# Attention backward on one core: the last 104 heads taken in pairs, with 16 KB rows in the transfers

## The chip, the core and the metric

The kernel runs on one core of one Trainium2 chip. The metric is device time in microseconds, the median of several executions: 1704.82 us for the kernel before. One core has TensorE (PE), VectorE (DVE), ScalarE (ACT), GpSimd (POOL) and a sync engine (SP) that here does nothing but issue transfers; 16 DMA engines move data between memory (HBM) and the on-chip buffer (SBUF), which has 128 partitions.

## What is computed

A decoder block with one query token for each of 4 sequences, forward, and then the gradients of all inputs. Cut to what matters:

```python
# B=4, H=32, Sk=4096, Dh=128: 128 heads (b, h), each with K and V of 4096 x 128 bf16 = 1 MB
q = layernorm(x) @ wq
p = softmax(q @ K^T * Dh**-0.5)           # one row of 4096 for each head
o = p @ V
h = x + o @ wo
out = h + swiglu(layernorm(h), w1, w3, w2)
# backward, for each head, with dO (1 x 128) from grad_out:
dV = outer(p, dO)                          # 4096 x 128, 1 MB
dP = dO @ V^T                              # needs V again
dS = p * (dP - sum(dO * o)) * Dh**-0.5     # one row of 4096
dK = outer(dS, q)                          # 4096 x 128, 1 MB
# and dx, d_wq, d_wo, d_w1, d_w2, d_w3
```

Both cache gradients are outer products of a column of 4096 and a row of 128, so the kernel writes 256 MB of dK and dV and reads K once and V twice, 384 MB.

## The kernel before, in words

A head is numbered s, with b = s % 4 and h = s // 4. In SBUF a head lies as 128 partitions x 32 rows of 128 elements: partition p has cache rows 32p to 32p+31, 8 KB in one run, so a transfer of one head is 128 rows of 8 KB. All large buffers come from one `arena` of 23 slots of 8,320 bytes a partition. `Slot` takes the first of the list `free`, `give` puts it back at its end; both happen while the program is written, so the list decides which earlier transfer a new user of a slot has to wait for. `Slot2` takes two neighbouring slots, for the 2 MB stores of weight gradients.

The forward part fills about the first 680 us. It streams K and V (L155, L163), keeps the probabilities in `P_all` (for each head 32 values a partition) and some sums for each head in the `M` slots, of which there are 8 when the backward part begins.

The backward part is one loop over s. Its order is written by hand; each engine takes its instructions in that order, and SP issues its transfers one after the other, each when its semaphores allow. In one step of the loop:

- `load_ahead(s + L)` (L1233) and `prefetch` (L1209) issue V loads (L810). V uses a ring `vring` of 7 slots; a load goes out as soon as a ring slot has been given back.
- `front(s + L)` (L1166), five heads ahead: 32 PE transposes of V (L777) in 4 groups, each evacuated by ACT onto the place of V (L778); then 8 matmuls (L1182) with dO in one column of a window `zd` of zeros, which GpSimd sets (L1147). Four heads share an accumulator `dP_ps`. At the next head after four `rows_out` copies it (L1157) and `rows_T` transposes it (L1164).
- `more_V(s + 1 + lead_V(s))`: dV of heads up to 8 ahead of s, from head 56 on gradually fewer, to 3. `grad_V` (L790) takes a slot, lets DVE write the outer product (`outer`, L783) and stores it (L794). Its inputs are the row dO, replicated on all partitions by PE and ACT four heads at a time (`replicate`, L1133 and L1136), and P with each value twice, side by side, from GpSimd (`P_pairs`, L1152).
- `grad_K(s)` (L1202): the same for dK, store L1206. Its column comes from `group_dS` (L1190) on DVE, once for four heads: four small subtractions (L1196) and one product with P (L1199).
- one or two units of other work (`step`): first the rest of dO (`rest_of_dO`), then one dq matmul for each head (`dq_work`), which gives back the M slots one by one, and from s = 35 on `side_work`: dx and the weight gradients, whose seven stores of about 2 MB (L1045) take 16 KB or 14 KB a partition.

The core of the slot and of one store:

```python
class Slot:
    def __init__(self, name, src=free):
        self.i = src.popleft()
...
def grad_K(s):
    gk = Slot("gk")
    outer(gk.heads(), dS2s[s // B][:, s % B], reps["rq", s // REP][:, s % REP, :])
    nc.sync.dma_start(out=rows_of(out_2[b, h]), in_=gk.heads())
    gk.give()
```

Of the kernel before, what the change touches and what calls it, by code (L numbers as in the profile page):

```python
# [9 lines left out]
FP32 = mybir.dt.float32  # L10
# [9 lines left out]
JQ = 8  # L20
NPE = 1


@with_exitstack
def kernel(
# [79 lines left out]

    free = deque(range(NSLOT))
    arena = slotp.tile([P, NSLOT * SLOT], BF16, name="arena")

    class Slot:
        def __init__(self, name, src=free):  # L110
            self.i = src.popleft()
            self.t = arena[:, self.i * SLOT:(self.i + 1) * SLOT]
# [10 lines left out]
        def give(self):  # L123
            free.append(self.i)

    class Slot2:
        def __init__(self):
            at = {i: n for n, i in enumerate(free)}
            self.i = min((max(at[i], at[i + 1]), i) for i in free if i + 1 in at)[1]
            free.remove(self.i)  # L130
            free.remove(self.i + 1)
            self.t = arena[:, self.i * SLOT:(self.i + 2) * SLOT]
# [673 lines left out]
    def load_V2(eng=nc.sync):  # L806
        s = nv["next"]
        if s < NH:
            V2s[s] = Slot("V2", vring if vring else free)
            eng.dma_start(out=V2s[s].heads(), in_=cache_head(A_v_cache, s))  # L810
            nv["next"] += 1
# [128 lines left out]
    with ExitStack() as c2:  # L940
# [204 lines left out]
        def dO_window(s):  # L1145
            if s < NH:
                nc.gpsimd.tensor_copy(out=zd[s % B][:, 32:132:67], in_=dOT_bf[:, s:s + 1].to_broadcast([P, 2]))  # L1147

        def P_pairs(s):
            if s < NH and s not in P2s:  # L1150
                P2s[s] = bw3.tile([P, SJ, 2], BF16, tag="P2", name="P2")
                nc.gpsimd.tensor_copy(out=P2s[s][:], in_=P_all[:, s, :, None].to_broadcast([P, SJ, 2]))  # L1152
# [13 lines left out]
        def front(s):  # L1166
# [20 lines left out]
            sl = VTs.pop(s)  # L1187
            (vring if len(V2s) + len(VTs) + len(vring) < NV2 else free).append(sl.i)

# [19 lines left out]
        def prefetch():  # L1209
            while nv["next"] < NH and vring:  # L1210
                load_V2(nc.sync)


        O0, S0, S1, L = 2, 21, 35, 5
        gvd = {"n": 2}

        def more_V(upto):
            while gvd["n"] < min(NH, upto):
                s = gvd["n"]
                P_pairs(s)  # L1220
                replicate("rdo", s - s % REP)
                grad_V(s)
                P_pairs(s + 1)
                P_pairs(s + 2)
                gvd["n"] += 1
                if s % REP == 2:
                    replicate("rdo", s + 2)

        def lead_V(s):
            return 8 - min(5, max(0, s - 56) // 4)  # L1230


        def load_ahead(s):  # L1233
            prefetch()
            if s < NH and s not in V2s and s not in VTs:
                load_V2(nc.sync)

        for s in range(2):
            dO_window(s)
# [11 lines left out]
        group_dS(0)  # L1251
        for s in range(NH):
            load_ahead(s + L)
            if s % REP == 2:
                replicate("rq", s + 2)
            if s + L < NH:
                front(s + L)
            elif s + L == NH:
                rows_out()
                rows_T()  # L1260
            if s > 0:
                more_V(s + 1 + lead_V(s))
            grad_K(s)
            if s % B == B - 1 and s + 1 < NH:
                group_dS((s + 1) // B)
            if O0 <= s < S0:
                step("o")
            if s >= S1:
                step("s", 2)
            elif s >= O0:  # L1270
                step("q")
        step("s", 400)
# [30 lines left out]
```

## Time and profile before

| | |
|---|---|
| time | 1704.82 us, three runs from 1703.26 to 1705.42 |
| profiled span | 1701.5 us |
| busy | PE 1235.3, DVE 1236.1, ACT 969.0, POOL 377.3 us |
| moved | 707.50 MB, HBM read 422.59 MB, written 282.34 MB |
| DMA packets on the main queue | 100,144 |
| outer products on DVE (L783) | 2292 ns each |
| evacuation of V groups on ACT (L778) | 1026 ns each, 512 of them |

The page gives for each engine the busy time, then the span in 40 equal slices with a busy digit for each engine, the DMA engines' mean busy share and the rate in GB/s. A share just over 1 for DMA means that packets of one engine overlap slightly. Groups of instructions stand with their count, busy time, mean duration, and the idle time of the engine just before them with what ended it. A busy PE is not a PE at its peak. For a transfer, "to landing" is the time from its issue by SP to its completion.

### The profile page before, as it was taken

The numbers are of one execution on the slowest core, as the hardware profiler recorded it, in microseconds if no ns is written. First come the engines' busy times: TensorE is split into PE (matmuls) and PEld (weight loads), VectorE is DVE, ScalarE is ACT, GpSimd is POOL, SyncE is SP. The second block draws the span as 40 slices with busy tenths as digits, with TensorE's granted clock in tenths as the row PEclk, the third lists the DMA queues.
The fourth block names the chain that finished last, engine by engine and source line by source line (L and its number), as shares of the span: only waits on it lengthen the run. The fifth ranks groups of instructions, "written<-read, shape, count | busy, mean of one in ns | idle before, by whom it ended". The sixth has DMA issues, their size and how long they took to land. (4 is left out here: it accounts for less than half of the span.)

```text
span 1701.5 us, 38421 instructions
## 1 busy us (share of the span) xinstructions
PE 1235.3 (73%) x16180; PEld 913.6 (54%) x16180; DVE 1236.1 (73%) x1294; ACT 969.0 (57%) x1502; POOL 377.3 (22%) x678
## 2 busy tenths in 40 slices
PE   5889888888888888878877664676557666766650
PEld 4777776667666766655655443444334343434430
DVE  5989999999999987667776666664457555665682
ACT  3555444544454444776666564677457865766540
POOL 1211222222222221233341111141114121200020
PEclk9999999999999999999999897979787977787775
DMA  9999999999999999999999999999999999999996
GB/s 401 424 424 424 424 424 424 424 423 424 417 423 412 424 405 400 385 420 424 425 426 425 425 426 425 425 426 427 423 425 420 417 422 412 414 416 420 411 424 275
DMA packets 100733, 707.50 MB, mean 416 GB/s; under 512 B 10940, under 2 KB 15176, under 8 KB 16720
## 3 DMA queue, kind: packets, MB, share of 16 engines
q1 hardware_dynamic: 100144, 704.95, 99.4%
q8 instruction: 127, 2.08, 0.5%
q14 instruction: 46, 0.38, 0.1%
q0 software_dynamic: 416, 0.10, 0.0%
HBM read 422.59 MB, written 282.34 MB: 414 GB/s over the span
## 5 line engine op out<-in xcount | busy, mean ns | idle before, releaser
L778 ACT COPY arena<-pt_tps 128x1024 bf16<-128x1024 bf16 x512 | 490.2, 1026 | 185.5 <-PE pt_tps L777 178.9
L777 PE MATMUL pt_tps<-ident_b,arena 128*128 128x128 bf16 x4096 | 351.6, 246 | 199.9 <-ACT arena L778 112.7
L777 PEld LDWEIGHTS <-arena 128*128 128x128 bf16 x4096 | 299.4, 112 | 274.5 <-issue 151.4
L783 DVE TENSOR_TENSOR arena<-P,arena 128x4096 bf16<-128x4096 bf16 x125 | 286.3, 2292 | 196.5 <-DMA out_dram<-arena 178.2
L783 DVE TENSOR_TENSOR arena<-dS,arena 128x4096 bf16<-128x4096 bf16 x128 | 293.1, 2292 | 119.1 <-DMA out_dram<-arena 118.3
L449 PE MATMUL M_ps<-arena 128*128 128x130 bf16 x4096 | 286.6, 223 | 37.6 <-DMA arena<-in_A_v_cache_dram 37.1
L434 DVE TENSOR_TENSOR arena<-arena 128x4096 bf16<-128x4096 bf16 x128 | 292.5, 2285 | 25.3 <-POOL arena L430 25.3
L449 PEld LDWEIGHTS <-arena 128*128 128x128 bf16 x4096 | 253.6, 99 | 58.2 <-DMA arena<-in_A_v_cache_dram 50.5
L341 DVE STREAM_TRANSPOSE arena<-arena 128x512 f32<-128x512 f32 (+1 forms) x321 | 250.5, 797 | 0.0
L336 ACT COPY arena<-pt_tps 128x1024 bf16<-128x1024 bf16 x128 | 129.4, 1012 | 186.4 <-PE pt_tps L335 148.8
L1182 PE MATMUL dP_ps<-arena,zd 128*32 128x512 bf16 x1024 | 175.7, 420 | 71.1 <-ACT arena L778 67.9
L1152 POOL COPY P<-P_all 128x64 bf16<-128x64 bf16 x125 | 82.1, 657 | 523.2 <-DVE arena L783 512.9
L1147 POOL COPY zd<-dOT_bf 128x2 bf16<-128x2 bf16 x128 | 123.4, 966 | 121.8 <-PE dP_ps L1182 121.8
L347 POOL TENSOR_TENSOR W<-qrep,wmask 128x128 bf16<-128x128 bf16 x128 | 120.8, 944 | 85.2 <-PE S_ps L367 70.4
L430 POOL COPY arena<-P_all 128x64 bf16<-128x64 bf16 x128 | 32.4, 253 | 413.8 <-ACT P_all L424 410.8
L1182 PEld LDWEIGHTS <-zd 128*32 128x32 bf16 x1024 | 37.0, 94 | 158.1 <-issue 144.1
L424 ACT COPY P_all<-pt_P 32x64 bf16<-32x64 bf16 x256 | 51.9, 203 | 55.6 <-PE pt_P L420 53.4
L953 ACT CAST arena<-gps 128x512 bf16<-128x512 f32 x110 | 62.7, 584 | 33.0 <-PE gps L959 29.3
L335 PE MATMUL pt_tps<-ident_b,arena 128*128 128x128 bf16 x1024 | 80.6, 224 | 0.0
L459 PE MATMUL kP_ps<-arena,onesw 128*32 128x512 bf16 x1024 | 79.2, 386 | 0.0
L335 PEld LDWEIGHTS <-arena 128*128 128x128 bf16 x1024 | 62.0, 100 | 25.8 <-issue 25.8
L413 ACT ACTIVATE Pn<-E,rl 128x1024 bf16<-128x1024 f32 x64 | 73.7, 1151 | 3.2 <-DVE rl L410 3.2
(226 smaller groups left out, 1190.6 us busy)
## 6 DMA issues: line engine op xcount, KB each, us to landing
arena<-in_A_v_cache_dram SPq DMA_DIRECT2D x256, 1024.0 KB, 18.3
out_dram<-arena SPq DMA_DIRECT2D x256, 1024.0 KB, 20.1
arena<-in_A_k_cache_dram SPq DMA_DIRECT2D x128, 1024.0 KB, 15.5
arena<-in_A_wq_dram SPq DMA_DIRECT2D x8, 1024.0 KB, 15.5
out_dram<-arena SPq DMA_DIRECT2D x4, 2048.0 KB, 22.8
arena<-in_B_w_dram SPq DMA_DIRECT2D x8, 896.0 KB, 15.1
out_dram<-arena SPq DMA_DIRECT2D x3, 1792.0 KB, 22.3
arena<-in_A_wo_dram SPq DMA_DIRECT2D x4, 1024.0 KB, 12.3
```

What stands on the lines that cost most here:

```text
L335: nc.tensor.transpose(pt[:, i, :], Kn[:, c * GW + i, :], ident_b[:])
L336: nc.scalar.copy(out=KT[:, c * GW:(c + 1) * GW, :], in_=pt[:])
L341: nc.vector.transpose(out=KT[:, c * w_:(c + n) * w_], in_=Kn[:, c * w_:(c + n) * w_])
L347: nc.gpsimd.tensor_tensor(out=W[:, hl], in0=qrep[:, :, s:s + 1].to_broadcast([P, 4, 32]), in1=wmask[:, hl, None, :].to_broadcast([P, 4, 32 ...
L434: nc.vector.tensor_tensor(out=PK[:, :, 0:Dh].rearrange("p j (r t) -> p j r t", t=2), in0=Ks[s].heads().rearrange("p j (r t) -> p j r t", t=2),
L449: nc.tensor.matmul(hold["M"][:], lhsT=Vn[:, j, :], rhs=PK[:, j, :], start=(j == 0), stop=(j == SJ - 1))
L777: nc.tensor.transpose(pt[:, i, :], v[:, g * GW + i, :], ident_b[:])
L778: nc.scalar.copy(out=v[:, g * GW:(g + 1) * GW, :], in_=pt[:])
L783: nc.vector.tensor_tensor(out=dst.rearrange("p j (r t) -> p j r t", t=2), in0=col2[:, :, None, :].to_broadcast([P, SJ, Dh // 2, 2]), in1=r ...
L1147: nc.gpsimd.tensor_copy(out=zd[s % B][:, 32:132:67], in_=dOT_bf[:, s:s + 1].to_broadcast([P, 2]))
L1152: nc.gpsimd.tensor_copy(out=P2s[s][:], in_=P_all[:, s, :, None].to_broadcast([P, SJ, 2]))
L1182: nc.tensor.matmul(rows["acc"][32 * c:32 * (c + 1), :], lhsT=zq_window(zd[hl], 2 * hl + u), rhs=VT[:, j0:j0 + 4, :], start=(hl == 0 and u ...
```

## The change

From head 24 on (`SP = 24`) two heads h and h+1 of the same b, which are neighbours in memory, are taken as one: partitions 0 to 63 hold the first head, 64 to 127 the second, 64 cache rows each. A V load, a dV store and a dK store are then one transfer of 2 MB with 16 KB a partition. That makes half as many transfers, with packets of twice the size; it also makes half as many outer products, of twice the length. To serve them:

- `Slot2` is used for V, dV and dK of a pair. It takes neighbours from a run of free slots in a way that leaves no odd slot over, and in the backward part single slots are taken from odd runs or the ends of runs (`lone_slot`).
- V loads go through `load_pairs`, up to 3 pairs ahead, in place of the ring.
- `front_pair` transposes 64 blocks in 8 groups and makes 16 matmuls for a pair; the accumulator holds two pairs.
- P has to be had in the new rows: `P_rows` brings it there with matmuls against every other column of the identity, for 4 pairs at a time, into a new slot `Pp`, which also holds the dO windows and the doubled P.
- `replicate_pair` fills partitions 0 to 63 with the row of one head and 64 to 127 with that of the other; `group_dS_pair` forms dS of two pairs.
- dV leads dK by 8 heads, from head 56 on gradually fewer, to 4.

```diff
+SP = 24
...
+    def lone_slot():
+        at = {i: n for n, i in enumerate(free)}
+        runs = runs_of_free()
+        odd = [e for r in runs if len(r) % 2 for e in (r[0], r[-1])]
+        i = min(odd or [e for r in runs for e in (r[0], r[-1])], key=lambda e: at[e])
+        free.remove(i)
+        free.appendleft(i)
...
+        def two_heads(ap, t):
+            b, h = t % B, H0 + t // B * 2
+            return ap[b, h:h + 2].rearrange("h (p j) d -> (h p) (j d)", p=P // 2)
+
+        def load_pair():
+            t = npv["next"]
+            npv["next"] += 1
+            pV[t] = Slot2()
+            nc.sync.dma_start(out=pV[t].t[:, 0:2 * SJ * Dh], in_=two_heads(A_v_cache, t))
+
+        def load_pairs(t):
+            while npv["next"] < NT and (npv["next"] <= t or len(pV) < 3 and len(Slot2.choices()) > 1):
+                load_pair()
...
+        def grad_pair(out_ap, t, col2, row):
+            g_ = Slot2()
+            outer_pair(g_.t[:, 0:2 * SJ * Dh], col2, row)
+            nc.sync.dma_start(out=two_heads(out_ap, t), in_=g_.t[:, 0:2 * SJ * Dh])
+            g_.give()
...
-            return 8 - min(5, max(0, s - 56) // 4)
+            return 8 - min(4, max(0, s - 56) // 4)
...
-        for s in range(NH):
+        for s in range(SP):
...
+        for t in range(NT):
+            s = SP + 2 * t
+            load_pairs(t + LP)
+            if t % B == 2:
+                replicate_pair("rq", t // B + 1)
+            if t + LP < NT:
+                front_pair(t + LP, lambda: side(s))
+            else:
+                if t + LP == NT:
+                    rows_out()
+                    rows_T()
+                side(s)
+            more_V(s + 2 + lead_V(s))
+            grad_pair(out_2, t, pdS[t // 2][:, t % 2], reps["rq", "p", t // B][:, t % B, :])
+            if t % 2 == 1 and t + 1 < NT:
+                group_dS_pair((t + 1) // 2)
+            side(s + 1)
```

## The prediction

> **What bounds the kernel now.** I read the table of slices first: which resource is full from end to end? In both rows below one column is a fortieth of the span, 42.5 us.
>
> ```profile
> DMA  9999999999999999999999999999999999999996
> GB/s 401 424 424 424 424 424 424 424 423 424 417 423 412 424 405 400 385 420 424 425 426 425 425 426 425 425 426 427 423 425 420 417 422 412 414 416 420 411 424 275
> ```
>
> The 16 DMA engines are full in 39 of 40 slices; no compute engine is (PE and DVE 73%, ACT 57%). 707.5 MB at 425 GB/s are 1665 us, so 40 us of the 1705 are lost: a dip around slices 14 to 17 (the forward part ends), a lower rate from slice 30 on, and the last slice. Next, the same counters in stretches of the backward part (columns: PE, PEld, DVE, ACT, POOL busy, clock, DMA share, GB/s):
>
> ```profile
> 735.00:870.00 135.00, 106.97 (x1211) 78.89 (x1209) 98.59 (x76) 96.78 (x111) 45.27 (x43) 0.94 1.01 425
> 870.00:1250.00 380.00, 241.56 (x2479) 162.58 (x2480) 223.48 (x166) 234.20 (x280) 74.88 (x99) 0.86 1.01 425
> 1250.00:1640.00 390.00, 261.12 (x2319) 164.93 (x2318) 246.62 (x169) 258.40 (x326) 70.02 (x105) 0.81 1.01 417
> 1640.00:1684.00 44.00, 10.32 (x88) 7.24 (x88) 25.55 (x17) 8.88 (x10) 2.38 (x2) 0.63 1.01 427
> 1684.00:1700.00 16.00, 0.00 (x0) 0.00 (x0) 0.00 (x0) 0.00 (x0) 0.00 (x0) 0.50 0.14 59
> ```
>
> The DMA share is 1.01 up to 1684 us and then 0.14: for the last 14 us about one engine of 16 works. The landing marks in the trace (16 for each transfer, one an engine) say the same: of the last transfer 15 are there by 1687.0 us, the last at 1700.2. They show one engine falling behind steadily from 735 us on, to 15 us by 1225, where it stays. So the end is set by the one slowest DMA engine, busy without a gap. An edit is worth what it takes out of that engine's packets, less the time in which it finds nothing queued.
>
> Who waits for what? DVE's outer products (out<-in, count | busy, mean ns | idle before, releaser), then the DMA issues, then the issuing queue:
>
> ```profile
> L783 DVE TENSOR_TENSOR arena<-P,arena 128x4096 bf16<-128x4096 bf16 x125 | 286.3, 2292 | 196.5 <-DMA out_dram<-arena 178.2
> L783 DVE TENSOR_TENSOR arena<-dS,arena 128x4096 bf16<-128x4096 bf16 x128 | 293.1, 2292 | 119.1 <-DMA out_dram<-arena 118.3
> ...
> arena<-in_A_v_cache_dram SPq DMA_DIRECT2D x256, 1024.0 KB, 18.3
> out_dram<-arena SPq DMA_DIRECT2D x256, 1024.0 KB, 20.1
> ...
> out_dram<-arena SPq DMA_DIRECT2D x4, 2048.0 KB, 22.8
> ```
>
> ```profile
> 1658.68 0.33 SPq L1206 DMA_DIRECT2D out_dram<-arena  x1
> 1661.13 0.33 SPq L794 DMA_DIRECT2D out_dram<-arena  x1
> ```
>
> DVE waits for stores to leave their slots, not the reverse. A transfer goes out every 2.47 us (1 MB at 425 GB/s) and lands 20.1 us later: eight are in flight. That is the program's own limit: it has 8 completion marks and takes them in turn, so transfer n waits for n-8.
>
> **The Trainium skill.** DMA: Bandwidth & Descriptors, section Why small descriptors are slow: the engine adds a fixed few cycles for each packet, whatever its size. The packet records of this trace agree (ns for one packet; queue 1):
>
> ```
> bytes   packets  10%  median  90%   mean
>  8192     82944  309     309  309  312.7
> 16384       512  611     611  611  621.7
> ```
>
> Two packets of 8 KB take 618 ns, one of 16 KB 611: 7 ns fixed. The same page, section Why a DMA increments its semaphore by 16 and not by 1: a transfer is complete only once all its engines have landed. Hence a slot comes free at the pace of the slowest engine, as in the 15 us above. SBUF — State Buffer, section The DMA setup-cost knee: about 2 us for each transfer beside its bytes. The shortest wq load here lands 4.9 us after issue, 2.4 more than its bytes need. Only the chain load, compute, store pays this, not a full queue.
>
> **The change part by part.**
>
> 1. Packets. Heads 24 to 127 are 52 pairs; each has one V load, one dV and one dK: 156 transfers of 2 MB in place of 312 of 1 MB. On each engine 8 packets of 611 ns and one completion mark of 9 replace 16 of 309 and two of 9: 4897 for 4962 ns, 65 less. From rates it is less: a 1 MB transfer takes 2464 ns, 19 less than its records add up to, since packets overlap by some 2 ns; so two take 4928, and the large one some 4880, 48 less. 156 x 48 to 65 ns = 7.5 to 10.1; I take **-8.7 us**. The trace has no 16 KB load, only stores (L1045); I take a load to cost the same, between 611 and 618.
> 2. Engine work. Transposes, the evacuation L778, the dP matmuls and the DVE elements stay the same in number. A pair's outer product is one instruction of at most 2 x 2292 = 4.58 us. Replication (L1136, 0.59 us each) halves on ACT; GpSimd's P copies go from two to one per pair. A pair needs 9.2 us of DVE (and 0.6 for its share of dS) and 8.2 us of L778 in 14.8 us of transfers (6 MB): no engine becomes the bound. New: 26 matmul sets for P in paired rows, one small evacuation per 4 pairs. All beside full DMA queues: 0.
> 3. Buffers while single heads still run. To keep neighbouring slots free, single buffers now come from odd leftovers. In the order of the changed program dV and dK of heads 2 to 7 each use one slot over and over (slots 0 and 2), reused 3 transfers later; before it was 6. A slot's loop is then landing, DVE 2.29, issue 0.3, latency 2.4, transfer 2.47 = 7.5 us and some semaphore time against 7.4 us for three transfers: 0.1 to 0.6 us lost per head for about 5 heads, **+1 to 3**. At the switch (heads 20 to 23) two dK again have distance 3, and after them DVE does dS (1.15), dK (2.29) and the first paired dV (4.58): 8 us in which 5 us of transfers are queued, **+1 to 3**. I take +2 for both, the lower ends, since the queue holds paired V loads as well.
> 4. Buffers in the paired part. Of 23 slots, 2 are fixed, the weight gradients hold 6 to 8, 13 to 15 are left: 6 or 7 pairs. The order shows stores and loads reusing slots mostly 4 to 7 transfers later (once 3). With distance 4, when a slot lands, three transfers or 14.8 us remain queued, and the refill takes 4.58 + 0.3 + 2.4 = 7.3: 7.5 us spare. The added wait: SP issues in order, so a paired V load that waits for its slot holds the dV and dK stores behind it, and DVE, which waits for their slots. V has 3 pairs in turn: 44.5 us for a round, of which PE and ACT need some 13 (8 evacuations of 1.03, then 16 matmuls), so a load may take 29 us to land, 5 transfers ahead of it. The queue is shorter: 0.
> 5. Start and end: the last store is 2 MB; DVE needs 4.58 for what DMA takes 4.9 for, so the queue stays filled; dV ends 2 pairs ahead of dK (before 3 heads). 0.
>
> Sum: 1704.8 - 8.7 + 2 = **1698 us**.
>
> **Rivals.** (B) The slow engine gains more. Since 735 us it has moved 3055 packets' worth in 965 us, 316 ns each; less some 8 us of instruction fetches (16 KB each, 49 of them in this stretch, spread over 8 engines, each a step of 1.3 us in the landing marks), 313 for 308 elsewhere. If those 5 ns are per packet, halving 2496 packets saves 6 us more; if the lower rate after 1250 us goes as well, up to 7 more: about 1690. Against: the slow engine's few 16 KB packets are late by some 15 ns each, twice the amount, which speaks for bytes. (C) The saving is given back: slot distances of 4 lie under the 8 of before, and each wait of DVE for the evacuation of a V slot takes from the spare 7.5 us; 0.12 us in each of 52 steps is 6: 1704. (D) Too few pairs of neighbouring slots: the queue runs dry at dS steps. dS for two pairs waits for the transposed rows, on PE behind the next pair's V load; if each of 26 steps exposes 0.7 us (five small DVE operations take 1.15), that is 18: 1716, slower. For it: the longest DVE wait for a store is 11.6 us already. Against: heads 24 on had no gap at 1.01 share.
>
> **How the numbers follow.** Forecast 0.50 (1695 to 1703; 0.45 of it faster by over 3.4 us, 0.05 the same), B 0.17 faster, C 0.17 (0.15 same, 0.02 slower), D 0.16 slower. Faster 0.62, same 0.20, slower 0.18. The range runs from below B (1687) to within D (1713), leaving out some 0.09 at each end.
>
> **What would show it.** Right: 19,968 packets of 16 KB more and 39,936 of 8 KB fewer, 16 KB loads at 611 ns, the rate in the paired stretch up from 425 and 417 by about 1%, one engine alone at the end. Step 3 is wrong if the share stays 1.01 from 735 to 900 us; step 4 if it falls below 0.98 after 900 us with DVE waiting for stores or V evacuations. The prediction fails if a 16 KB load costs over 618 ns or SP stands behind V loads with empty queues.

## The result and the profile after

The changed kernel takes 1730.81 us (1730.15 to 1733.15) beside 1704.27 us (1703.26 to 1705.42) for the kernel before: a ratio of 1.016, 95% interval 1.014 to 1.018, 26.5 us slower. The forecast was 1698, with 1687 to 1713 as range.

First the table of slices of the kernel after. Its columns are 43.3 us wide.

```profile
DMA  9999999999999999699989999999999999999997
GB/s 401 424 425 424 424 423 425 423 423 424 417 420 407 424 413 401 251 385 385 427 362 425 430 427 428 428 426 430 426 396 406 427 419 401 414 407 401 402 406 337
DMA packets 78264, 707.45 MB, mean 409 GB/s; under 512 B 8444, under 2 KB 12680, under 8 KB 14224
```

Three things are seen. In the slices where the backward part is settled (the 22nd to the 29th) the rate is 425 to 430, mostly a little above the 425 of before: that is the gain that was looked for. Against it stands a hole of 251 GB/s in the 17th slice, with 385, 385 and 362 soon after. And from the 30th slice on the rate is mostly between 400 and 415. The same in stretches (columns: PE, PEld, DVE, ACT, POOL busy, clock, DMA share, GB/s), after and then before:

```profile
690.00:735.00 45.00, 33.45 (x448) 24.92 (x447) 21.79 (x23) 27.74 (x33) 7.26 (x23) 0.81 0.65 261
735.00:860.00 125.00, 84.35 (x930) 62.35 (x926) 71.91 (x56) 73.77 (x85) 22.03 (x36) 0.85 0.99 396
860.00:910.00 50.00, 39.70 (x428) 30.73 (x426) 39.68 (x27) 32.50 (x38) 3.05 (x5) 0.80 0.91 372
910.00:1280.00 370.00, 237.21 (x2468) 177.28 (x2468) 222.42 (x122) 229.97 (x274) 64.97 (x54) 0.78 1.01 427
1280.00:1310.00 30.00, 21.85 (x260) 14.57 (x256) 20.05 (x11) 24.67 (x31) 8.78 (x4) 1.00 0.93 369
1400.00:1690.00 290.00, 180.03 (x1580) 126.02 (x1579) 176.85 (x83) 171.58 (x216) 31.51 (x31) 0.69 1.00 406
```

```profile
690.00:735.00 45.00, 33.35 (x457) 23.87 (x455) 32.03 (x31) 30.23 (x37) 15.95 (x27) 0.92 0.96 382
735.00:860.00 125.00, 99.70 (x1134) 74.23 (x1132) 88.87 (x71) 89.37 (x103) 37.87 (x38) 0.93 1.01 425
860.00:910.00 50.00, 37.76 (x412) 26.56 (x412) 38.43 (x27) 34.05 (x40) 18.16 (x20) 1.00 1.01 425
```

A rate that is short by d of R over a stretch of w us costs d/R x w. The first stretch costs 121/425 x 45 = 12.8 us, the second 8.5, the third 6.2. Those three make 27.5 us, and all lie before the paired part has settled. From 1280 to 1310 us 3.9 are lost (before: 424 GB/s), and from 1400 us on 6.3 against the 415 GB/s that the kernel before has up to 1640 us. The settled stretches, from 910 to 1280 and 1310 to 1400 us, give back 3.0. At the end one DMA engine works alone for 7.4 us instead of 13.2 (landing marks of the last transfer), which gives back 5.8. The sum is 28.9; the two profiled spans differ by 29.9.

DVE's outer products of pairs and the transfers, from the page after:

```profile
L1355 DVE TENSOR_TENSOR arena<-arena 128x8192 bf16<-128x8192 bf16 x52 | 230.0, 4423 | 183.9 <-DMA out_dram<-arena 168.3
L1355 DVE TENSOR_TENSOR arena<-dS,arena 128x8192 bf16<-128x8192 bf16 x52 | 230.0, 4425 | 120.9 <-DMA out_dram<-arena 120.7
...
out_dram<-arena SPq DMA_DIRECT2D x108, 2048.0 KB, 21.5
...
out_dram<-arena SPq DMA_DIRECT2D x48, 1024.0 KB, 8.1
```

A paired product takes 4.42 us, below the 4.58 assumed, so no engine has become the bound. The last line is the sign of trouble: the 48 stores of 1 MB of the first 24 heads land 8.1 us after issue, where a store took 20.1 before. A short landing time means that little was queued ahead. In the queue's own waits, SP stands for the product:

```profile
SPq L1365 <- DVE arena L1355: 686.9, 103, 16.6
...
SPq L820 <- DVE arena L809: 81.0, 22, 9.5
```

Waits for the product stand in the kernel before too (44.0 us for its dV stores, in 24 waits), with a queue that stays full; whether one hurts is seen only from the DMA share beside it. In the timeline of DVE it does hurt. After, then before (start, us, operation, and in brackets the idle time ahead of it and who ended that):

```profile
700.32 2.28 DVE L809 TENSOR_TENSOR arena<-arena 128x4096 bf16<-128x4096 bf16 x1
...
710.22 2.29 DVE L809 TENSOR_TENSOR arena<-arena 128x4096 bf16<-128x4096 bf16 x1 [7.51 <-DMA out_dram<-arena]
716.51 2.29 DVE L809 TENSOR_TENSOR arena<-P,arena 128x4096 bf16<-128x4096 bf16 x1 [4.00 <-DMA out_dram<-arena]
722.80 4.49 DVE L809 TENSOR_TENSOR arena<-P,arena 128x4096 bf16<-128x4096 bf16 x2 [4.00 <-DMA out_dram<-arena]
```

```profile
707.11 2.29 DVE L783 TENSOR_TENSOR arena<-P,arena 128x4096 bf16<-128x4096 bf16 x1 [2.17 <-DMA out_dram<-arena]
709.58 2.29 DVE L783 TENSOR_TENSOR arena<-P,arena 128x4096 bf16<-128x4096 bf16 x1 [0.17 <-DMA out_dram<-arena]
712.07 2.29 DVE L783 TENSOR_TENSOR arena<-P,arena 128x4096 bf16<-128x4096 bf16 x1 [0.20 <-DMA out_dram<-arena]
```

Before, a product follows every 2.5 us, the time of 1 MB. After, every 6.3 us: 2.29 for the product and 4.00 until its own store has landed. The order of the program says why. Counted among SP's transfers from the start of the program (the first is number 0), numbers 280 to 285 are dV of heads 1 to 6, and five of the six use slot 0: heads 2, 3 and 4 each wait for the store just before, head 6 for the second before it. Only head 5 has another slot; its product is the second of the two in the line at 722.80. Before, heads 2 to 6 took three slots in turn. No V load lies between them.

A milder form follows, from transfer 291 to 309, where dV keeps to slot 0 and dK to slot 2, mostly three transfers after the last use. The products of dV for heads 13 and 14:

```profile
782.89 2.29 DVE L809 TENSOR_TENSOR arena<-P,arena 128x4096 bf16<-128x4096 bf16 x1 [3.21 <-DMA out_dram<-arena]
...
792.41 2.29 DVE L809 TENSOR_TENSOR arena<-P,arena 128x4096 bf16<-128x4096 bf16 x1 [3.93 <-DMA out_dram<-arena]
```

From head 10 to head 14 one such product follows the other in 8.5 us on average (7.1 to 9.5), and the bytes of the three transfers between them take 7.4.

At the switch to pairs the same view shows two more such waits, for dK of heads 15 and 16 (transfers 336 and 337, three transfers behind the last use of their slot):

```profile
858.92 2.29 DVE L809 TENSOR_TENSOR arena<-dS,arena 128x4096 bf16<-128x4096 bf16 x1 [7.48 <-DMA out_dram<-arena]
873.60 2.29 DVE L809 TENSOR_TENSOR arena<-dS,arena 128x4096 bf16<-128x4096 bf16 x1 [10.19 <-DMA out_dram<-arena]
```

Two 2 MB loads of V go out together just before (331 and 332), and then none until 343. The stores behind them depend on DVE alone.

### The profile page after: what moved, and what is told of

It reads as the page before. It is cut to its first block, busy times and chain, and to the rows that moved or that the text cites. A ratio compares the mean times of both kernels' runs of the same rounds, so it can differ in the third digit from the quotient of the medians.

```text
span 1731.4 us, 37799 instructions
## 1 busy us (share of the span) xinstructions
PE 1240.6 (72%) x16232; PEld 954.3 (55%) x16232; DVE 1231.9 (71%) x1190; ACT 959.4 (55%) x1489; POOL 318.3 (18%) x575
## 4 chain that ended last, share of the span: by engine, by line
DMA 41%; DVE 13%; issue 3%; PE 3%; ACT 1%; DVEq 0%; SPq 0%; POOL 0%; ACTq 0%
DMA out_dram<-arena 38%; DVE arena L1355 8%; DMA arena<-in_A_v_cache_dram 4%; DVE arena L809 3%; ACT arena L1275 1%; PE M_ps L475 1%; DVE arena L460 1%; PE pt_w L604 1%; PE pt_tps L1274 0%; ACT Pn L439 0%; DVEq L1493 0%; PE kP_ps L485 0%; DVE dPr L1302 0%; PE gu_ps L876 0%; PE dn_ps L907 0%
## 5 line engine op out<-in xcount | busy, mean ns | idle before, releaser
L1274 PE MATMUL pt_tps<-ident_b,arena 128*128 128x128 bf16 x3328 | 328.2, 269 | 223.8 <-DMA arena<-in_A_v_cache_dram 147.7
L1274 PEld LDWEIGHTS <-arena 128*128 128x128 bf16 x3328 | 282.1, 124 | 321.4 <-DMA arena<-in_A_v_cache_dram 168.9
L1355 DVE TENSOR_TENSOR arena<-arena 128x8192 bf16<-128x8192 bf16 x52 | 230.0, 4423 | 183.9 <-DMA out_dram<-arena 168.3
L1355 DVE TENSOR_TENSOR arena<-dS,arena 128x8192 bf16<-128x8192 bf16 x52 | 230.0, 4425 | 120.9 <-DMA out_dram<-arena 120.7
L475 PEld LDWEIGHTS <-arena 128*128 128x128 bf16 x4096 | 253.4, 99 | 55.7 <-DMA arena<-in_A_v_cache_dram 48.6
L1352 POOL COPY arena<-arena 128x128 bf16<-128x128 bf16 x52 | 78.1, 1502 | 562.3 <-ACT arena L1329 300.9
L1289 PE MATMUL dP_ps<-arena 128*32 128x512 bf16 x832 | 91.4, 473 | 9.2 <-ACT arena L1275 9.1
L803 PE MATMUL pt_tps<-ident_b,arena 128*128 128x128 bf16 x768 | 64.9, 244 | 32.9 <-ACT arena L804 27.9
L361 PE MATMUL pt_tps<-ident_b,arena 128*128 128x128 bf16 x1024 | 80.5, 223 | 0.0
L803 PEld LDWEIGHTS <-arena 128*128 128x128 bf16 x768 | 56.0, 112 | 41.3 <-issue 40.0
L809 DVE TENSOR_TENSOR arena<-P,arena 128x4096 bf16<-128x4096 bf16 x21 | 48.0, 2290 | 43.2 <-DMA out_dram<-arena 43.0
L809 DVE TENSOR_TENSOR arena<-dS,arena 128x4096 bf16<-128x4096 bf16 x24 | 54.9, 2295 | 31.6 <-DMA out_dram<-arena 31.5
```

Of the source, the lines that this page charges most:

```text
L475: nc.tensor.matmul(hold["M"][:], lhsT=Vn[:, j, :], rhs=PK[:, j, :], start=(j == 0), stop=(j == SJ - 1))
L803: nc.tensor.transpose(pt[:, i, :], v[:, g * GW + i, :], ident_b[:])
L809: nc.vector.tensor_tensor(out=dst.rearrange("p j (r t) -> p j r t", t=2), in0=col2[:, :, None, :].to_broadcast([P, SJ, Dh // 2, 2]), in1=r ...
L1274: nc.tensor.transpose(pt[:, i, :], v[:, g * GW + i, :], ident_b[:])
L1289: nc.tensor.matmul(rows["acc"][32 * c:32 * (c + 1), :], lhsT=zt[t % B][:, 32 - m:64 - m], rhs=v[:, j0:j0 + 4, :], start=(pl == 0 and u == ...
L1355: nc.vector.tensor_tensor(out=dst.rearrange("p (j r t) -> p j r t", r=Dh // 2, t=2), in0=col2[:, :, None, :].to_broadcast([P, 2 * SJ, Dh / ...
```

## Experiments: where the first 20 us went

Theory S: the rule for single slots (`lone_slot`), which is in force from the start of the backward part, makes the first holes. Rival P: pairs as such cost the time.

**The rule from head 12 on.** In the changed kernel:

```diff
-        part["B"] = True
         for s in range(2):
             dO_window(s)
...
         for s in range(SP):
+            if s == 12:
+                part["B"] = True
```

> The changed kernel, but single slots are taken first in, first out, as before, until head 12; from there as changed. Theory S (the new rule for single slots lets dV and dK of the first heads reuse one slot at distance 1 to 4, and DVE and the stores run in turn): the rate from 690 to 860 us returns to that of before, some 23 us come back, 1708 us. Rival P (the pairs themselves starve the queue, the start only hides it): under 8 us come back, 1723 us or more, with the idle DMA time moved into the paired part.

Measured: 1709.6 us, ratio to before 1.0035 (1.0022 to 1.0048). 21.2 us come back.

**The rule alone.** In the kernel before, no pairs, `lone_slot` as in the change:

```diff
+        part["B"] = True
...
         for s in range(NH):
+            if s == 12:
+                part["B"] = False
```

> The kernel before, without any pairs, but with the changed rule for single slots until head 12. Theory S: it is slower than before by the same 20 to 23 us, 1725 us, though no transfer has changed its size. Rival P: 1704 to 1708 us.

Measured: 1720.67 us, ratio 1.0098 (1.0083 to 1.0113): 16.6 us lost without a single pair. The two stretches of this run show the rates of the changed kernel:

```profile
690.00:735.00 45.00, 32.31 (x428) 23.82 (x425) 20.94 (x22) 26.69 (x32) 9.34 (x23) 0.81 0.67 264
735.00:860.00 125.00, 88.44 (x980) 65.00 (x978) 85.75 (x67) 79.34 (x91) 33.10 (x37) 0.88 1.00 397
```

S holds, from both sides, though the rule alone cost 16.6 us where 20 to 23 were expected. What is left is 5.5 us by which pairs are behind even so, and the question where the gain of the packets is.

## Experiments: the packets and the spacing of the loads

**Pairs with rows of 8 KB.** The run with the rule from head 12 on, with each partition's 16 KB in two pieces, in the halves of its two slots:

```diff
-            outer_pair(g_.t[:, 0:2 * SJ * Dh], col2, row)
-            nc.sync.dma_start(out=two_heads(out_ap, t), in_=g_.t[:, 0:2 * SJ * Dh])
+            for x in range(2):
+                outer(halves(g_.t)[:, x].rearrange("p (j d) -> p j d", d=Dh), col2[:, x * SJ:(x + 1) * SJ], row)
+            nc.sync.dma_start(out=half_rows(two_heads(out_ap, t)), in_=halves(g_.t))
```

> As e1, but each partition of a pair is moved as two pieces of 8 KB, the halves lying in the two slots with a gap between; transfers stay 2 MB and 156, the outer product of a pair becomes two instructions (4.58 for 4.42 us). Theory of the packet price (7 ns for each packet, 65 ns less for each 2 MB): 7.5 to 10 us more than e1. Rival (packets of 8 KB cost nothing where the queue is the limit, or the paired part is not limited by DMA): within 3 us of e1.

Measured: 1713.45 us, 3.9 more than the run with 16 KB: between the 7.5 to 10 of the theory and the 3 of the rival. In the settled stretch from 910 to 1200 us the rates are 429 and 426 GB/s; from 1400 us on there is no difference, 407 and 408. In this pair of runs packets matter only where the queue is full.

**V loads of pairs one at a time.** Again the run with the rule from head 12 on, and in the loop of single heads:

```diff
-            if nv["next"] >= SP:
-                load_pairs((s + L - SP) // 2)
+            if nv["next"] >= SP and npv["next"] < NT and npv["next"] <= (s + 3 - 18) // 2:
+                load_pair()
```

> As e1, but around the switch to pairs the paired V loads go out one every two heads, not two at once with a pause after. Theory (at the switch the queue holds stores alone for 40 us, which DVE cannot make at the DMA rate): 4 to 6 us less than e1, the DMA share from 860 to 910 us back at 1. Rival (the slot distances of 3 at the switch cost it, not the missing loads): within 2 us of e1.

Measured: 1700.55 us, ratio 0.998 (0.9974 to 0.9987), 9.1 less and 3.6 us faster than the kernel before, so pairs as such need not cost time. More than expected, and not where expected. The first line is the run above this edit started from, the second this one:

```profile
1290.00:1650.00 360.00, 228.98 (x2004) 158.69 (x2004) 209.81 (x100) 219.99 (x281) 36.39 (x48) 0.69 1.00 411
```

```profile
1290.00:1650.00 360.00, 231.66 (x2049) 161.41 (x2047) 226.67 (x108) 222.74 (x284) 69.82 (x49) 0.69 1.01 429
```

The switch got better (396 to 423 GB/s from 860 to 910 us) and the stretch ahead of it worse (419 to 404 from 735 to 860 us), but most of the gain is 400 us later. Since slots are dealt out from a list, an edit at the first loads of pairs deals the hand for the whole rest. Of the 80 transfers after number 430, 25 take up a slot with only 6 MB queued since its last transfer in the first run, and 5 in this one. That gave the next theory: slots too fresh.

**Older slots.** Two edits to who gets which slot; nothing else moves:

```diff
-        i = min(odd or [e for r in runs for e in (r[0], r[-1])], key=lambda e: at[e])
+        late = len(free) - 6
+        ends = [e for r in runs for e in (r[0], r[-1])]
+        old = [e for e in odd if at[e] < late]
+        i = min(old or (ends if len(Slot2.choices()) > 2 else odd or ends), key=lambda e: at[e])
...
-            if s == 12:
+            if s == 14:
```

and the slot of the second 2 MB store of weight gradients is given back one unit of side work later.

> The kernel of the run with the evenly spaced V loads, with two more edits in who gets which slot and none in what is moved or computed: a single head's slot is taken from the six last returned ones only if nothing else leaves a pair over, with the rule from head 14 on (12 before), and the slot of the second 2 MB weight-gradient store goes back one unit of side work later. In the queue's order no transfer from head 14 on then takes up a slot with less than 4 MB queued since the slot's last transfer, and after transfer 430 none with less than 8 MB. Theory 'slots too fresh': the two stalls left in the profile of that run, 118 and 50 GB/s short over 15 us each around 825 to 855 us and 37 GB/s short over 70 us from 1210 us on, are worth 5.9 and 6.1 us, and go: 1688.5 us, 1686 to 1692, and the DMA share stays at 1.00 or above from 735 to 1640 us. Rival 'the last engine': one DMA engine works alone over the last 13 us there, and if it is its own backlog that sets the end, filling the stalls of all sixteen only lengthens the time in which it is alone: 1697 to 1701 us.

> The same with the rule from head 12 on: up to transfer 430 about as before, but after it 15 transfers (of 80) take up a slot with only 6 MB queued since its last transfer, where the run beside it has none under 8 MB. Theory 'slots too fresh': 6 MB last 15 us at 425 GB/s, and a 2 MB slot needs some 5 us to be filled by the vector engine before and some 8 us to land behind what is ahead of it, so that the queue runs shallow; the stretch from 1400 to 1640 us, which ran at 407 GB/s in the changed kernel with its first 12 heads in rotation (25 such transfers) and at 429 with the V loads evenly spaced (5), runs at 412 to 420: 1693 to 1699 us. Rival: six MB is enough, and what slowed that stretch was something else (the V loads' spacing, or what the gaps before it left behind): within 2 us of the run beside it, 428 GB/s from 1400 us on.

> The run with the old slots with each partition's 16 KB in two pieces of 8 KB, in the halves of its two slots, and two outer products of 4096 elements in place of one of 8192: packet sizes as in the kernel before, everything else of the change in place. Theory 'price right, but paid only where the queue is full': the queue is full now through the whole paired part, so that the whole price shows, 104 transfers at 64 us for 128 packets' difference each: 7 to 9.5 us more than the run beside it, and about 425 GB/s against 428 from 900 us on. Rival: it was 3.9 us in the pair of runs before because the last engine or the fixed times hide the rest: 3 to 5 us more.

Measured: 1708.88 us (1707.41 to 1713.73), 1709.27 (1704.97 to 1710.98) and 1717.46 (1711.06 to 1719.07). In the third expectation the working should read 156 transfers at 48 to 65 ns. The first two missed. In the second run the stretch from 1400 to 1640 us did come in the range given (414 GB/s), yet the time is that of the run beside it. The third came as given, 8.6 us more, but not for the reason given: from 910 to 1200 us the rates are 426 and 427 GB/s, and the difference lies in the late stalls (408 against 416 from 1290 to 1650 us). In the first run the early stalls did go (425 GB/s from 735 to 860 us, 430 to 910), and others came:

```profile
1170.00:1290.00 120.00, 85.07 (x745) 58.02 (x744) 61.64 (x35) 76.90 (x96) 14.67 (x14) 0.69 0.99 403
...
1440.00:1650.00 210.00, 127.78 (x1148) 89.86 (x1147) 127.65 (x63) 124.32 (x156) 43.69 (x25) 0.71 1.00 407
```

A version with fewer fresh slots and fewer early stalls is 8 us slower than one with both. With 15 reuses at 6 MB the late stretch is 406 GB/s from 1290 to 1530 us and 428 from there to 1620; without, 423 and 406. So freshness alone is not the cause. The 8.6 us between the first and the third run mix the packets with stalls that fall differently, and say nothing certain about either.

## Experiments: the late engine

What was left out is something that the prediction had read and not used: one DMA engine lags. For each transfer the trace has 16 landing marks, one an engine. The largest distance from first to last mark, in us, in windows of 30 us from the time given (by the last mark), from the trace:

```
              780  1050  1080  1200  1260  1500  1620
before        3.1  11.4  12.3  15.1  15.8  16.0  15.9
after         3.0   5.2   5.9   8.7   8.5  10.0  10.0
rule from 12  3.4   5.7   6.4   9.5   8.1  10.1  10.3
even V loads  3.2   6.5   7.4  10.5   8.3  10.4  14.0
old slots     3.2  11.8  12.7  13.3  10.1  15.5  17.5
```

In the backward part the lag grows by some 0.8 us in 30 us, falls where a hole in the queue lets the late engine catch up, and stays at a ceiling. In the changed kernel and with the rule from head 12 on the ceiling is 10 us, with many reuses at 6 MB; with old slots, at 8 MB after transfer 430, it is 15 to 17. This fits simple arithmetic: 6 MB last 14.8 us at 425 GB/s, less the 4.4 that DVE needs to fill the slot again, 10.4; 8 MB last 19.7, less 4.4, 15.3. A slot comes back when the late engine has landed its part (the Trainium skill, DMA: Bandwidth & Descriptors, section Why a DMA increments its semaphore by 16 and not by 1, says that only all engines together complete a transfer; the marks agree). At the ceiling the other fifteen run out of work: that is the theory, and the trace shows of it the ceilings and, at the same time, lower rates.

Theory L: the late engine sets the end; a hole in the queue costs only what is longer than the fall of its lag; at the ceiling the fifteen stop and start together. Two tests in the kernel before, with a hold-up of DVE that leaves the result the same:

```diff
+        for again in range(14 if s == 52 else 0):
+            outer(gv.heads(), P2s[s], reps["rdo", s // REP][:, s % REP, :])
         outer(gv.heads(), P2s.pop(s), reps["rdo", s // REP][:, s % REP, :])
```

> The kernel before, with the outer product of head 52's dV done 15 times in place of once (the same result): the vector engine is busy for 32 us more at about 1050 us, in a stretch at 426 GB/s. Nothing else differs. The question is what one gap in the queue costs. Theory 'the gap is all': the engines of the DMA run dry after the 8 to 20 us that are queued, stand for 12 to 24 us, and then go at 425 GB/s at once: the time is up by the gap, and in the 15 us windows after it the packets take as long as before. Theory 'restart': as sixteen engines start again in step, the packets after the gap are slower, 1.5 to 2 us of extra packet time per engine in the 15 to 20 us that follow, on top of the gap. A third way: the kernel before has slack that takes up part of the gap, as its end is set by one late engine that has 14 us of its own work left: the time is up by the gap less up to 10 us.

> The kernel before with its hold-up at the dV of head 12, about 765 us, in place of head 52 at 1050 us; the same 32 us of vector work, which cost nothing there (1703.7 against 1704.5 us). Theory 'late engine': at 765 us the late engine is only 2 to 3 us behind, so of a gap of 5 to 7 us it works through 2 to 3 and then stands idle with the others: 3 to 6 us longer, 1707 to 1711 us, and the lag at the end is as in the kernel before. Rival 'slack of the vector engine': the kernel makes up for a hold-up of the vector engine wherever it falls, since that engine has time to spare in each head: 1703 to 1705 us, as at head 52.

Measured: 1703.73 us at head 52, ratio 0.9997 (0.9988 to 1.0005), and 1730.62 us at head 12, ratio 1.0153 (1.0139 to 1.0167). The same 32 us of vector work cost nothing at one place and 26.5 us at another. Of the first expectation the third way came, with the slow packets of the second. At head 52, then at head 12:

```profile
1050.00:1080.00 30.00, 21.59 (x239) 16.56 (x238) 29.69 (x14) 19.92 (x23) 7.38 (x4) 0.87 0.87 351
1080.00:1110.00 30.00, 21.40 (x240) 13.73 (x239) 29.83 (x26) 20.91 (x24) 19.32 (x10) 0.93 1.01 413
```

```profile
750.00:810.00 60.00, 31.64 (x344) 24.68 (x344) 55.30 (x37) 25.57 (x29) 14.23 (x10) 0.77 0.57 225
```

At head 52 the hole is 6.1 us (5.2 and 0.9) and the lag falls from 11.8 to 4.5: the late engine works through it. At head 12 the hole is 28.2 us, not the 5 to 7 expected, since the queue there ran dry 10 us into the hold-up; the lag could fall only from 3.0 to 1.2. That expectation failed in its size. So most of the difference between the two places is the size of the hole; what the lag explains is the rest, the 6.8 and 1.7 us by which each time is below its hole. After the first hole the second line shows 413 GB/s at a share of 1.01, engines busy but slow: in the 15 us from 1075 us on the packets took 1.8 us an engine longer than the medians of their sizes, against 0.1 in the windows around. A restart is not free.

**The pause in the changed kernel.** If L holds, a pause should cure the kernel with old slots. There, the product of the 14th pair's dV is made eight, six or four times, or the 20th's six times, or the 14th's and the 34th's eight times each:

```diff
             g_ = Slot2()
+            for again in range(7 if out_ap is out_3 and t in (14,) else 0):
+                outer_pair(g_.t[:, 0:2 * SJ * Dh], col2, row)
             outer_pair(g_.t[:, 0:2 * SJ * Dh], col2, row)
```

> The run with the old slots, with the vector engine held up once: the product of the 14th pair's dV is made eight times in place of once (the same result), 31 us more of vector work at about 1050 us. Theory 'late engine': one DMA engine falls behind the other fifteen by 0.8 to 1 us in 30 us (in the completion marks of the run with the old slots from 3 us at 780 us to 13.5 us at 1110 us), a slot comes back only when that engine has ended with it, and once it is as late as the time that a slot has until its next turn, the fifteen run dry, start again together and pass slow packets. A gap shorter than the lag costs nothing, since the late engine works through it, and takes the lag down: here from 12 to 4 or 5 us. The stall at 1200 to 1290 us (391 to 410 GB/s) goes, 418 or above from 1100 to 1400 us, and the stretch after it is as before or better. The kernel gets faster by added work: 1697 to 1704 us against 1708.9. Rival 'a gap is a gap': the queue runs dry for 5 to 10 us and nothing gives them back: 1714 to 1720 us.

> The same with a second hold-up of 31 us, at the dV of the 34th pair, about 1350 us. Theory 'late engine': the lag is taken down twice, never reaches the 15 us that a slot with 6 MB queued behind it gives, and no stall is left from 860 us on but the two gaps themselves, which the late engine works through. The late engine then works at the 417 to 420 GB/s that it shows wherever no burst of slow packets falls (414 to 416 in the kernel before with 8 KB packets), without a break from 735 us on: the 965 us that it works in the kernel before become 954 to 958, and the bursts after the two gaps add up to 2 us each: 1690 to 1697 us. Rival 'a gap is a gap': two gaps of 5 to 10 us: 1719 to 1729 us.

> The same as the run with two pauses, with each partition's 16 KB in two pieces of 8 KB and two products of 4096 elements for one of 8192 (the repeated ones too). Theory 'late engine and price right': with the late engine busy throughout, the time is its packets, and the whole price of the small packets shows: 156 paired transfers of 2 MB at 48 to 65 ns each is 7.5 to 10 us more than the run beside it. Rival: the price is hidden, as in the two pairs of runs before it where stalls of other origin covered or enlarged it: 0 to 5 us more.

Measured: 1706.72 us (ratio to before 1.0017, 1.001 to 1.0023), 1720.49 (1.0093, 1.0077 to 1.0108) and 1725.74 (1.0125, 1.0111 to 1.0139). All three missed what L gave; the second lies in the range of the rival 'a gap is a gap', with holes of some 20 us in place of the rival's 5 to 10, and the third, 5.2 us above the second, between theory and rival. The late stalls are gone, as L says, but the holes were twice as long as the lag. The run with one pause:

```profile
1049.64 35.64 DVE L1365 TENSOR_TENSOR arena<-arena 128x8192 bf16<-128x8192 bf16 x8 [6.43 <-DMA out_dram<-arena]
```

```profile
1050.00:1110.00 60.00, 29.42 (x336) 23.29 (x333) 59.65 (x19) 28.41 (x33) 17.62 (x5) 0.74 0.73 297
1110.00:1400.00 290.00, 197.14 (x1782) 135.72 (x1780) 176.43 (x95) 190.16 (x241) 63.10 (x44) 0.73 1.01 429
1170.00:1290.00 120.00, 82.91 (x775) 56.17 (x775) 65.80 (x36) 79.65 (x101) 17.69 (x13) 0.76 1.01 429
...
1440.00:1650.00 210.00, 129.34 (x1164) 91.54 (x1164) 133.82 (x64) 125.60 (x157) 44.30 (x25) 0.71 1.01 428
```

So a reset of the lag and a plain loss were mixed. Three more runs take them apart.

> The run with one pause, with the product of the 14th pair's dV made six times in place of eight: 22 us of added vector work, 9 less. In the profile of the run with one pause the queue was dry from about 1067 to 1086 us; here it is dry for about 9 us, just the lag of the late engine (9.5 us at 1050 us). Theory 'late engine': that engine works through the gap, the lag falls to 1 to 2 us, and the late stalls do not come, 428 GB/s from 1110 us on: 9 us less than the run with one pause, 1696 to 1700 us, faster than the kernel before. Rival 'the pause cures by something else and costs its gap': 1702 to 1706 us. Rival 'a gap is a gap': 1714 us.

> The same with the product made four times, 13 us of added vector work: 18 us less than in the run with one pause, whose queue was dry for 18 us, so that the queue just doesn't run dry here. Theory 'late engine': no gap, no reset; the lag goes on to 13 us at 1150 us and the stalls from 1170 us on come as in the run without a pause: 1705 to 1710 us. Rival 'other cure' (that the vector engine falls back by some us, or the order in which slots come back, is what helps, and not the gap): 1696 to 1702 us.

> The pause of six products at the 20th pair, about 1140 us, where the lag of the late engine is 13 us in the run without a pause. Theory 'late engine': a gap of about 9 us costs nothing there either, takes the lag to about 4 us, and from there it grows by 0.8 us in 30 us to 13 or 14 us at 1550 us and stays at the edge for the last 100 us: 1696 to 1702 us. Rival 'a gap is a gap': 1714 us or more.

Measured: 1697.51 us (ratio 0.9959, 0.9947 to 0.9972), 1708.07 (1.0021, 1.0011 to 1.0031) and 1705.15 (1.0008, 1.0000 to 1.0016). The short pause, 22 us of added vector work, makes the kernel 11.4 us faster than without, 10.6 faster than the too short one beside it, and 6.4 faster than the kernel before; it is the fastest of all. The one of 13 us, which hardly empties the queue, changes nothing. Short pause, then too short:

```profile
1050.00:1110.00 60.00, 34.09 (x397) 26.74 (x393) 59.51 (x26) 31.78 (x36) 17.62 (x5) 0.78 0.85 348
...
1170.00:1290.00 120.00, 84.31 (x776) 56.69 (x773) 65.63 (x36) 81.39 (x103) 18.59 (x15) 0.74 1.01 429
...
1440.00:1650.00 210.00, 131.51 (x1173) 93.22 (x1173) 135.50 (x64) 126.05 (x158) 42.39 (x23) 0.70 1.01 429
```

```profile
1050.00:1110.00 60.00, 36.41 (x414) 28.99 (x414) 54.50 (x33) 34.75 (x40) 14.85 (x9) 0.81 0.99 410
...
1170.00:1290.00 120.00, 83.18 (x752) 57.71 (x751) 61.80 (x36) 78.44 (x99) 16.47 (x14) 0.74 0.99 411
...
1440.00:1650.00 210.00, 130.58 (x1144) 93.08 (x1142) 126.69 (x61) 124.25 (x156) 42.62 (x25) 0.68 0.99 404
```

These two also show what makes the stall from 1170 to 1290 us. Transfers 419 to 428 contain seven that take up a slot with 6 MB queued since its last use, in the same order in every run with old slots. In the too short run they come at a lag of 11.9 us, above the 10.4 of the arithmetic: the rate drops (the 411 GB/s above) and the lag falls to 8.9. After the short pause they come at a lag of 3.3 us, and the rate is 429. From 1620 to 1650 us that run has a lag of 14.4 us again, but no slot with only 6 MB queued, and the rate stays at 427. So it is not the fresh slots alone and not the lag alone, but a lag longer than the slots leave time for.

The later pause missed its range: its hole was 20.9 us, not 9. All seven pauses on one sheet. "Hole" is the shortfall in the 60 us around it (against 425 GB/s in the kernel before, 428 to 429 with old slots), "fall" that of the lag, both from the trace; the fourth column is hole less fall; the fifth, where late stalls went away, takes off 13 us for them, one number for all three, set by the short pause:

```
                        hole  fall  hole-fall  less 13  measured   against
head 52, before          6.1   7.3    -1.2       -       -0.7      before
head 12, before         28.2   1.8    26.4       -      +26.5      before
too short               2.5    3.3    -0.8       -       -0.8      old slots
short pause             11.2   9.7     1.5     -11.5    -11.4      old slots
one pause               18.4   8.8     9.6      -3.4     -2.2      old slots
later pause             20.9  11.6     9.3      -3.7     -3.7      old slots
second of two pauses    20.7   6.7    14.0       -      +13.8      one pause
```

The four rows without the 13 agree within 0.5 us and have nothing fitted. In the other three the 13 is fitted to the short pause, and the later pause and the one pause come within 0.1 and 1.2 us of it. It is not what the stalls themselves take: by the rates (403 and 407 against 429 GB/s, in the lines above) these are 7.3 and 10.8 us, and part of the fall is lost again, as the lag grows after the pause. The rule was worked out after most of the runs; what was said ahead is the short pause and the one too short, and both came as L said.

**The packets again.** With two pauses the queue is full outside the holes, and 8 KB against 16 KB rows differ by 1725.74 - 1720.49 = 5.2 us. From 1110 to 1400 us, 16 KB and then 8 KB:

```profile
1110.00:1400.00 290.00, 199.49 (x1777) 135.23 (x1775) 176.28 (x95) 190.94 (x242) 61.44 (x44) 0.71 1.01 429
```

```profile
1110.00:1400.00 290.00, 202.49 (x1777) 139.58 (x1775) 176.88 (x130) 188.74 (x239) 50.23 (x44) 0.69 1.01 426
```

0.7% in rate. The packets themselves differ by 1.0%: 613.9 ns on average for 16 KB, 620.2 for two of 8 KB (1120 to 1400 us). The rest comes back between packets: added up without rounding, their records cover 1.007 of the time with 16 KB and 1.011 with 8 KB, so the smaller ones overlap more.

## Why the prediction was wrong

**What bounds the kernel.** Right as far as the runs go: with the late engine busy throughout, a hole costs nothing (head 52), and where it has nothing queued the time is lost (head 12). The prediction wrote that sentence and then did not work with it in steps 3 and 4.

**Step 1, packets, -8.7 us.** The mechanism is right: 19,968 packets of 16 KB more and 39,936 of 8 KB fewer, 611 ns each in the 10th percentile and the median, for loads too. The size is off: 5.2 us in the pair of runs with a full queue, below the 7.5 given as the lower end. (The 19 ns in its working should be 17: 2481 less 2464; nothing hangs on it.) In the changed kernel less was earned still, as its queue is not full from 1280 us on.

**Step 2, engine work, 0.** Right: with a paired product of 4.42 us DVE is busy 60% of the stretch from 910 to 1280 us, and no engine has taken the place of DMA. TensorE's granted clock was lower, 0.847 against 0.899 in the profiled runs, but the short pause, at 0.848, is faster than the kernel before, so that did not cost the time.

**Step 3, buffers while single heads still run, +2 us.** The step that failed. It measured 21 us up to 860 us by the rates, shown twice (21.2 us back without the rule in the first 12 heads, 16.6 lost by the rule alone), and 6 at the switch. Two things in it were wrong. First the reading of the order: it gave dV of heads 2 to 7 a distance of 3, but they take up their slots 1, 1, 1, 13, 2 and 3 transfers after the last use; 3 holds for dV of heads 10 to 14 and dK of heads 1 to 6. At distance 1 nothing is queued behind the slot, and the loop of 6.3 us stands against 2.5 for the bytes of one transfer. Second the loop at distance 3: it was put at 7.5 us and measured 8.5, so that each turn loses 1.1 us and not 0.1 to 0.6. The sign that the prediction named, a share below 1.01 from 735 to 900 us, was there, though the largest hole lay before 735 us.

**Step 4, buffers in the paired part, 0 us with 7.5 us spare.** Wrong. The spare time was counted from a slot's landing as if all engines landed together. The lag of 10 us and more eats it: that is the ceiling of 10.4 us for 6 MB. The sign named for this step, a share below 0.98, showed after 910 us only around 1280 us (0.93), where a product waited 19 us for the slot of a weight-gradient store. That is the one reuse at distance 3 that the step mentions and puts at nothing; the stretch lost 3.9 us. In the late stretch it stayed at 1.00; the loss there is in the packets, which take 644 ns on average from 1440 to 1650 us in the changed kernel against 614 with the short pause. A DMA share of 1.00 does not say that the engines move what they could.

**Step 5, start and end, 0.** The engine that works alone at the end does so 5.8 us less, since holes have let it catch up; the other side of the same loss.

**The rivals.** B (the late engine gains more, as its extra time is per packet) did not come: in the two runs with two pauses its lag grows as much with packets of 16 KB as with 8 KB, by 6.2 and 6.0 us from 1110 to 1410 us. C put the loss where slots are reused at distance 4, and that is where the late stretch loses; without the first holes the change stands at 1709.6, past C's 1704. D had the right sign, and for the most part the wrong place: not the dS steps of pairs, but the single heads.

What stays open: what makes that one engine slower by some 0.8 us in 30 (the records do not name the engines), and why packets take longer after a restart. Neither was tried. That slots dealt differently move the late stalls is shown, and that a hole which takes the lag down removes them; that the ceiling is the queued megabytes less DVE's filling time is arithmetic that fits at two sizes, no more, and that the fifteen stop and restart there is argued from the slow packets.

## What to carry to other kernels

When the rule for dealing out buffers changes, list the reuse distance of every transfer from the first at which the rule is in force, and count the queued megabytes against the landing of the slowest engine, not of the mean one. Where a kernel is bound by transfers, look at all 16 landing marks: here, with one engine lagging, a hole in the queue cost only what was longer than the fall of its lag. A change to the stores of one part deals the buffers of all later parts anew, so compare stretch by stretch before crediting it with a difference in time.

## What was not expected of the hardware

- In the backward part of the kernel before, one of 16 DMA engines falls behind by about 0.8 us in each 30 us, up to 16 us, and ends the kernel 13 us after the others.
- A hold-up of 32 us on the vector engine cost 0 or 26.5 us, by where it fell; one of 22 us made a kernel 11.4 us faster.
- After the queue has run dry, packets are slow for up to 15 us: they took 1.8 us an engine longer after the pause at head 52 (372 GB/s from 1075 to 1090 us) and 2.0 after the short pause, and the DMA share stayed at 1.00.
